# Zeros of 64 columns before the first K product, keys of 12 tiles summed on VectorE, and a new order, in a one-core linear-attention block with an MLP

## The chip, the cores and the metric

The kernel runs on one core of one Trainium2 chip. The metric is the device time of one execution in microseconds (us); lower is better. The five engines of the core each work through a queue of their own, in order: TensorE (PE, with its weight loads PEld), VectorE (DVE), ScalarE (ACT), GpSimd (POOL) and SyncE (SP), which issues all the DMAs here. Times inside an execution are counted from the start of its span.

## The reference

Input x is 2048 rows of 512 values in bfloat16. There are 32 heads of 16.

```python
def phi(t): return where(t > 0, t + 1, exp(t)) + 1e-6
u = layernorm(x)                          # over the 512 values of a row
q, k, v = split(u @ wqkv)                 # wqkv 512 x 1536
kv  = einsum("bhsd,bhse->bhde", phi(k), v)
z   = sum over s of phi(k)
o   = (phi(q) @ kv) / (phi(q) . z + 1e-6)
h   = x + o @ wo
out = h + relu(layernorm(h) @ w1) @ w2    # w1 512 x 1792, w2 1792 x 512
```

## The kernel before

The 2048 rows are 16 tiles of 128 rows; four tiles make a chunk c of 512 rows. Everything stays in SBUF. One string, ORDER (lines 18 to 53), fixes the order of the whole program: each word names a piece of work and its numbers, and the last loop of the kernel (lines 528 to 530) calls the function `op_<name>` with them. Words of one engine stand in that engine's queue in the order of the string; between engines only data count. There is no loop over tiles, and no scheduler.

The words that matter below (t a tile, c a chunk, b a PSUM bank):

- `lx.t.n` loads n tiles of x, `lk lq lv lo l1 l2` load parts of the weights (lines 200 to 211), all from SP's queue.
- `const` (line 173) sets constants on DVE, among them the zeros, and makes the identity on POOL; `masks` (186) makes masks on POOL. `warm.n.b` (213) multiplies zeros by zeros n times into bank b, 512 columns each, and nobody reads the result.
- `S.t`, `A.t` (218, 219): row statistics of x on DVE. `R.t.n` (238): 1/sqrt(variance) on ACT. `N.t` (241): normalized rows on DVE.
- The normalized tile is transposed in one of two ways. `T.t.b` (265) does it on PE, and `E.t` (ACT, 271) or `V.t` (DVE, 274) copies the result out of PSUM; `X.t` (283) does it with a DMA transpose. Tiles 0 to 3 take the first way, 4 to 15 the second.
- `K.t.b` (287): keys of tile t, 4 matmuls of 128x512. `F U M D` (329 to 332) make phi of them: exp and relu on ACT, a minimum and an add on DVE. `G.t` (341) adds u.T @ phi(k) of tile t into banks 4 to 7; v is never computed, its weights come in later.
- The sum z of the keys over all rows: `za.t` (348) adds the phi(k) of two tiles to an accumulator in float32 on DVE (1024 columns each time), `zf` (352) folds the two halves and splits them into two bfloat16 parts, and `z.j.b.t0` (358) sums over rows on PE by products with a column of ones: the two parts and the tiles t0 to 15, which were not added on DVE. `zc`, `zh` (367, 370) bring z to the form in which `dn` uses it.
- `Q.c.j.b` (296): queries of chunk c, with phi by `qF qU qM qD`. `gA`, `gD` (375, 378) copy the sums of G out of PSUM on ACT or DVE, `kv`, `kx` (381, 390) and `m` (394) turn them into one 512x512 matrix m, which `mA` or `mD` (398, 401) copies out.
- For each chunk a chain: `dn.c` (435, PE) the denominators, `dnl`, `dnx` (445, 451, ACT) their inverse spread over the heads, `dt.t` (458) four DMA transposes into rd, `dm.c` (462, DVE) phi(q) times rd, `h.t` (470, PE) times m, `hD` (479, DVE) plus x, `s a n` (220, 221, 249) the second layernorm's statistics and centred rows, `x.t` (284) four DMA transposes of these (hn) into lnT.
- The MLP: `p.c.f.b` (486, PE) a first product of 4 matmuls, `pA` or `pD` (495, 500) relu of two of them on ACT or DVE, `f.t.b.f0.n` (506, PE) n matmuls of the second product, `fo` (516, DVE) scale and add of h, `fd` (523) the store.

PSUM has 8 banks, and every word names its own.

Of the kernel before, what the change touches and what calls it, by code (L numbers as in the profile page):

```python
# [28 lines left out]
zc G.12 qD.0.0.2 G.13 zh dn.0.0 G.14 G.15 dnl.0 dnx.0.2.2 gD.0.2 Q.1.0.2 Q.1.1.3 dnx.0.0.2 gA.2.2 kv.0.4
Q.1.2.0 kv.3.4 Q.1.3.1 kv.2.4 qF.1.0.2 qU.1.0.2 qM.1.0.2 lo.2.2 lo.0.2 kv.1.4 kx Q.2.1.3 qF.1.2.2 dt.2 dt.3  # L30
dt.0 dt.1 qU.1.2.2 m.0.4 m.1.5 m.3.7 m.2.6 Q.2.0.2 qM.1.2.2 mA.0.2 qD.1.0.2 qD.1.2.2 dn.1.5 mA.2.2 dnl.1
dnx.1.2.2 dm.0.0.2 dm.0.2.2 h.3.4 h.2.0 hD.3 s.3 l1.0.2 dnx.1.0.2 hD.2 dt.6 a.3 Q.2.3.1 h.0.5 s.2 dt.4 hD.0
qU.2.0.2 qF.2.0.2 Q.2.2.0 qM.2.0.2 h.1.2 dt.5 dt.7 s.0 n.3 a.2 hD.1 a.0 s.1 n.0 Q.3.1.3 a.1 n.2 qF.2.2.2
qU.2.2.2 qM.2.2.2 dm.1.0.2 Q.3.0.2 dm.1.2.2 n.1 Q.3.3.1 Q.3.2.0 x.3 qF.3.0.2 qU.3.0.2 h.7.4 h.6.5 x.0 x.2
qU.3.2.2 qD.2.2.2 x.1 qD.2.0.2 dn.2.3 dnl.2 qF.3.2.2 h.5.6 h.4.7 hD.7 qM.3.0.2 hD.6 hD.5 s.7 p.0.0.2 p.0.1.3
hD.4 qM.3.2.2 s.6 dnx.2.2.2 dnx.2.0.2 pD.0.0.2 qD.3.2.2 s.4 dt.10 p.0.3.1 p.0.2.0 p.0.4.2 p.0.5.3 pA.0.2.2
pA.0.4.2 qD.3.0.2 dt.8 dt.11 dt.9 dn.3.6 p.0.6.0 p.0.7.1 p.0.13.3 dnl.3 s.5 a.4 p.0.12.2 pA.0.6.2 dnx.3.0.2
pA.0.12.2 r.0.4 dnx.3.2.2 l2.0.7 a.5 n.5 a.7 dm.2.0.2 a.6 n.6 dm.2.2.2 n.7 x.7 h.11.4 h.9.6 h.8.1 h.10.5 hD.11
n.4 hD.9 hD.8 hD.10 x.4 dt.13 dt.12 x.6 x.5 dt.14 dt.15 p.0.10.0 f.2.6.0.7 p.0.11.1 pA.0.10.2 p.0.8.2 p.0.9.3
f.3.7.0.7 pD.0.8.2 s.8 dm.3.0.2 dm.3.2.2 f.2.6.7.7 p.1.0.0 p.1.1.1 f.3.7.7.7 h.12.3 pD.1.0.2 h.14.4 p.1.2.2  # L40
p.1.12.0 hD.12 s.12 fo.3 fo.2 s.10 a.12 s.9 hD.14 s.11 a.9 n.9 h.13.7 f.1.5.0.7 p.1.13.1 h.15.3 a.10 hD.13 a.8
n.10 pD.1.12.2 n.8 hD.15 s.15 p.1.10.6 p.1.11.7 f.0.4.0.7 p.1.3.3 p.1.8.0 f.0.4.7.7 a.15 p.1.9.1 fd.2
f.1.5.7.7 pD.1.2.2 s.13 n.15 pA.1.8.2 fo.1 a.11 n.12 n.11 pD.1.10.2 x.8 x.9 x.10 x.11 p.1.4.0 p.1.5.1 p.1.6.2
r.4.4 p.1.7.3 pA.1.4.2 pA.1.6.2 f.5.5.0.7 p.2.3.3 p.2.8.0 p.2.9.1 f.7.7.0.7 p.2.2.2 pD.2.8.2 fo.0 p.2.1.1
p.2.0.0 f.6.6.0.7 s.14 a.13 n.13 pD.2.2.2 pD.2.0.2 a.14 p.2.7.3 f.4.4.0.7 p.2.12.0 p.2.6.2 f.7.7.7.7 p.2.13.1
n.14 f.5.5.7.7 pD.2.6.2 pA.2.12.2 p.2.5.1 p.2.4.0 x.13 fd.0 fd.3 x.15 fd.1 pA.2.4.2 x.14 x.12 f.4.4.7.7
p.3.0.0 p.3.2.2 p.3.1.1 f.6.6.7.7 p.3.3.3 pA.3.2.2 pD.3.0.2 fo.7 fo.5 fo.6 fo.4 p.3.9.1 f.11.7.0.7 p.2.11.3
fd.4 p.3.8.0 p.2.10.2 f.9.5.0.7 pD.2.10.2 pD.3.8.2 p.3.6.2 p.3.7.3 f.9.5.7.7 f.10.6.0.7 pA.3.6.2 p.3.10.2
p.3.11.3 f.8.4.0.7 fd.6 fd.5 fd.7 p.3.4.0 f.10.6.7.7 p.3.5.1 f.11.7.7.7 f.8.4.7.7 pA.3.4.2 r.12.4 r.8.4
pD.3.10.2 fo.9 fo.10 fo.8 fo.11 p.3.12.0 p.3.13.1 pD.3.12.2 fd.9 fd.8 fd.10 fd.11 f.14.6.0.7 f.13.5.0.7  # L50
f.12.4.0.7 f.14.6.7.7 f.13.5.7.7 f.12.4.7.7 fo.13 fo.14 fo.12 fd.12 fd.14 f.15.7.0.14.0.2 fo.15.0.2
f.15.4.0.14.2.1 f.15.5.0.14.3.1 fo.15.2.1 fo.15.3.1 fd.13 fd.15.0.2 fd.15.2.1 fd.15.3.1
"""


# [1 line left out]
def kernel(  # L57
# [155 lines left out]
    def op_warm(n, b):  # L213
        for _ in range(n):
            nc.tensor.matmul(bk[:, b, :], lhsT=zeros[:, 0:P], rhs=zeros, start=True, stop=True)
# [345 lines left out]
```

## Time and profile before

| | us |
|---|---|
| median of 3 runs | 171.17 |
| the three runs | 171.17, 172.66, 170.6 |
| the profiled execution | 171.47 |
| its span, first to last instruction | 169.8 |
| PE busy | 162.2 |
| DVE busy | 103.3 |
| ACT busy | 64.9 |
| POOL busy | 4.7 |
| time to the first K product | 7.30 |
| time to the first MLP product (p.0.0) | 62.62 |

The sizes of the pieces by the profile's groups (mean of one instruction): a row statistic on DVE 0.67, an aggregate 0.16, a normalization 0.40, a copy or relu of 128x1024 out of PSUM 1.22 on DVE and 1.02 on ACT, an add of 128x1024 into the accumulator 1.22. DMA transposes take a median of 2.5 us from issue to landing.

How to read it: a group's line gives engine, operation, shape, count, then busy time, the mean of one in nanoseconds, and the idle time before it with what ended most of it. A row of the order of time gives start, length, engine, line, names and count, with the idle time before it in brackets. A PE instruction's length holds its way through the array, so the distance from one start to the next, and not the length, is what it costs.

### The profile page before, as it was taken

The numbers are of one execution on the slowest core, as the hardware profiler recorded it, in microseconds if no ns is written. First come the engines' busy times: TensorE is split into PE (matmuls) and PEld (weight loads), VectorE is DVE, ScalarE is ACT, GpSimd is POOL, SyncE is SP. The second block draws the span as 40 slices with busy tenths as digits, with TensorE's granted clock in tenths as the row PEclk, the third lists the DMA queues.
The fourth block names the chain that finished last, engine by engine and source line by source line (L and its number), as shares of the span: only waits on it lengthen the run. The fifth ranks groups of instructions, "written<-read, shape, count | busy, mean of one in ns | idle before, by whom it ended". The sixth has DMA issues, their size and how long they took to land.

```text
span 169.8 us, 2263 instructions
## 1 busy us (share of the span) xinstructions
PE 162.2 (96%) x843; PEld 75.4 (44%) x858; DVE 103.3 (61%) x206; ACT 64.9 (38%) x97; POOL 4.7 (3%) x21
## 2 busy tenths in 40 slices
...
GB/s 144 251 253 95 94 95 184 262 359 60 99 174 165 93 66 85 152 173 86 92 6 31 31 62 29 2 0 107 113 0 0 70 54 4 0 0 124 0 4 120
DMA packets 32234, 15.87 MB, mean 93 GB/s; under 512 B 24800, under 2 KB 31200, under 8 KB 32224
## 3 DMA queue, kind: packets, MB, share of 16 engines
...
q8 instruction: 6, 0.10, 0.2%
q14 instruction: 4, 0.03, 0.1%
HBM read 7.86 MB, written 2.10 MB: 59 GB/s over the span
## 4 chain that ended last, share of the span: by engine, by line
PE 80%; DMA 6%; DVE 6%; SPq 2%; issue 2%; ACT 1%; DVEq 0%
PE bk L510 29%; PE bk L490 28%; PE bk L474 7%; PE bk L343 7%; PE bk L291 5%; PE bk L299 5%; DMA x_nat<-in_A_x_dram 3%; DMA lnT<-h_nat 2%; DVE h_nat L480 2%; DMA rd<-wk_sb 1%; SPq L201 1%; DVE st L220 1%; DVE h_nat L243 1%; PE bk L440 1%; ACT eb L309 1%
## 5 line engine op out<-in xcount | busy, mean ns | idle before, releaser
L510 PE MATMUL bk<-w_sb,at 128*128 128x512 bf16 (+2 forms) x249 | 51.9, 355 | 0.2
L490 PE MATMUL bk<-lnT,w_sb 128*128 128x512 bf16 x219 | 51.8, 379 | 0.2
L496 ACT ACTIVATE at<-bk 128x1024 bf16<-128x1024 f32 x13 | 13.3, 1024 | 70.6 <-PE bk L490 48.7
L501 DVE TENSOR_SCALAR at<-bk 128x1024 bf16<-128x1024 f32 x15 | 18.2, 1220 | 32.5 <-PE bk L490 32.3
L510 PEld LDWEIGHTS <-at 128*128 128x128 bf16 x252 | 23.6, 98 | 25.4 <-ACT at L496 0.3
L490 PEld LDWEIGHTS <-w_sb 128*128 128x128 bf16 x224 | 21.8, 98 | 26.1 <-issue 0.2
L518 DVE SCALAR_TENSOR_TENSOR gT<-bk,rstd,h_nat 128x512 bf16<-128x512 f32 (+2 forms) x18 | 11.7, 685 | 16.0 <-PE bk L510 10.5
L312 ACT ACTIVATE rb<-bk 128x1024 bf16<-128x1024 f32 (+1 forms) x18 | 16.4, 927 | 3.7 <-PE bk L299 2.4
L309 ACT ACTIVATE eb<-bk 128x1024 bf16<-128x1024 f32 (+1 forms) x18 | 16.6, 927 | 3.0 <-PE bk L299 2.8
L291 PE MATMUL bk<-wk_sb,lnT 128*128 128x512 bf16 x63 | 15.6, 379 | 1.3 <-DMA wk_sb<-in_A_wqkv_dram 0.6
L474 PE MATMUL bk<-m_sb,pqs 128*128 128x512 bf16 x61 | 15.0, 379 | 0.9 <-DVE pqs L464 0.8
L299 PE MATMUL bk<-lnT,wq_sb 128*128 128x512 bf16 x64 | 15.6, 379 | 0.2 <-DVE h_nat L480 0.2
L343 PE MATMUL bk<-at,h_nat 128*128 128x512 bf16 x54 | 13.3, 379 | 0.1
L480 DVE TENSOR_TENSOR h_nat<-bk,x_nat 128x512 bf16<-128x512 f32 x16 | 10.9, 681 | 2.0 <-PE bk L474 1.9
L218 DVE BATCH_NORM_STATS2 st<-x_nat 128x6 f32<-128x512 bf16 x16 | 10.6, 674 | 2.4 <-DMA x_nat<-in_A_x_dram 2.4
L220 DVE BATCH_NORM_STATS2 st<-h_nat 128x6 f32<-128x512 bf16 x16 | 11.0, 686 | 0.1
L291 PEld LDWEIGHTS <-lnT 128*128 128x128 bf16 x64 | 5.8, 98 | 9.5 <-DMA lnT<-h_nat 1.8
L474 PEld LDWEIGHTS <-pqs 128*128 128x128 bf16 x64 | 6.0, 98 | 8.0 <-DVE pqs L464 1.5
L299 PEld LDWEIGHTS <-wq_sb 128*128 128x128 bf16 x64 | 6.1, 98 | 7.2 <-issue 0.4
L343 PEld LDWEIGHTS <-h_nat 128*128 128x128 bf16 x64 | 6.1, 98 | 7.1
L316 DVE TENSOR_SCALAR eb<-eb 128x1024 bf16<-128x1024 bf16 (+1 forms) x18 | 6.8, 384 | 2.5 <-ACT eb L309 2.5
L453 ACT ACTIVATE wk_sb<-ld 128x1024 bf16<-128x1024 f32 x8 | 8.1, 1049 | 0.1
...
## 6 DMA issues: line engine op xcount, KB each, us to landing
...
```

Of the source, the lines that this page charges most:

```text
L220: op_s = lambda t: nc.vector.bn_stats(out=st2[:, t, :], in_=h_nat[:, t, :])
L291: nc.tensor.matmul(bk[:, b, :], lhsT=lnT[c][:, kd, j * P : (j + 1) * P], rhs=wk_sb[:, kd, :], start=(kd == 0), stop=(kd == KD - 1),)
L299: nc.tensor.matmul(bk[:, b, :], lhsT=wq_sb[:, kd, j * P : (j + 1) * P], rhs=lnT[c][:, kd, :], start=(kd == 0), stop=(kd == KD - 1),)
L309: nc.scalar.activation(out=buf(eb, kind, i, n), in_=bank(at_bank[kind, i], n), func=ACT.Exp)
L312: nc.scalar.activation(out=buf(rb, kind, i, n), in_=bank(at_bank[kind, i], n), func=ACT.Relu)
L343: nc.tensor.matmul(bk[:, KD + kd, :], lhsT=ln_nat[:, t, kd * P : (kd + 1) * P], rhs=pk(t)[:, 0, :], start=(t == 0), stop=(t == NT - 1),)
L474: nc.tensor.matmul(bk[:, b, :], lhsT=pqs[:, (c * KD + jb) % NQ, j * P : (j + 1) * P], rhs=m_sb[:, jb, :], start=(jb == 0), stop=(jb == KD ...
L480: nc.vector.tensor_tensor(out=h_nat[:, t : t + n, :], in0=bank(at_bank["h", t], n), in1=x_nat[:, t : t + n, :], op=ALU.add,)
L490: nc.tensor.matmul(bk[:, b, cols], lhsT=w1_sb[:, kd, f * P : (f + 1) * P], rhs=lnT[c][:, kd, cols], start=(kd == 0), stop=(kd == KD - 1),)
L496: nc.scalar.activation(out=acts[c % 2][:, f : f + n, :], in_=bank(at_bank["p", c, f], n), func=ACT.Relu)
L501: nc.vector.tensor_scalar(out=acts[c % 2][:, f : f + n, :], in0=bank(at_bank["p", c, f], n), scalar1=0.0, scalar2=None, op0=ALU.max,)
L510: nc.tensor.matmul(bk[:, b, 0 : w * P], lhsT=acts[c % 2][:, f, j * P : (j + 1) * P], rhs=w2_sb[:, f, k * P : (k + w) * P], start=(f == 0), ...
```

## The change

- New word `warms.n.b`: n products of zeros of 64 columns. 48 of them are added: 16 ahead of the ten long zeros, which stay, 16 behind them and ahead of the first transpose T.0, and 16 between T.0 and T.2.
- The accumulator on DVE takes 12 tiles in place of 14: `za.12` is gone, and the four `z` words start at tile 12, so that each has 6 products in place of 4.
- The order is new everywhere. At the start: the loads of x go 2, 1, 0, 4 and 5, 3 in place of 0, 2, 1, 3, 4 and 5; the transposes on PE go 0, 2, 1, 3 in place of 2, 0, 1, 3, and tile 2 is copied out by DVE (`V.2`) and not by ACT. The loads of the two halves of w1 swap places. `gA.2` becomes `gD.2`, `mA.2` becomes `mD.2`, and some relus of the MLP go from DVE to ACT or back. The banks are new, too.

```diff
-const lx.0.1 S.0 lx.2.1 S.2 lx.1.1 A.2 A.0 table warm.9.7 R.2.1 S.1 lx.3.1 N.2 A.1 R.0.1 R.1.1 N.0 lx.4.2
-warm.1.7 T.2.0 S.3 E.2 N.1 T.0.1 A.3 lk.0.2 lk.2.2 S.4 S.5 A.4 lx.6.2 A.5 T.1.5 E.0 R.3.1 E.1 R.4.2 lx.8.4 N.3
-K.0.3 S.6 N.4 F.0.1 U.0.1 K.1.0 lx.12.4 M.0.1 S.7 N.5 F.1.1 X.4 A.6 D.0.1 M.1.1 A.7 T.3.5 E.3 K.2.3 S.9 U.1.1
...
-K.14.2 K.15.3 qU.0.0.2 qF.0.0.2 za.10 G.9 za.12 Q.0.2.0 Q.0.3.1 F.14.2 l1.2.2 M.14.2 U.14.2 zf.12 qF.0.2.2
-D.14.2 G.10 G.11 z.0.2.14 z.2.2.14 z.1.2.14 qM.0.2.2 qM.0.0.2 z.3.2.14 qU.0.2.2 qD.0.2.2 lv.2.2 l2.7.7 lv.0.2
...
+lx.2.1 const lx.1.1 lx.0.1 S.2 S.1 A.2 masks S.0 A.1 table lx.4.2 A.0 lx.3.1 R.2.1 R.0.1 R.1.1 N.2 S.3 N.0 A.3
+S.4 N.1 S.5 lk.0.2 warms.8.2 warms.8.1 warm.9.7 warm.1.7 warms.8.3 warms.8.2 A.4 T.0.4 warms.8.1 warms.8.5
+T.2.0 R.3.1 A.5 E.0 T.1.6 V.2 lk.2.2 K.0.5 E.1 R.4.2 K.1.1 lx.6.2 N.3 S.7 N.5 A.7 N.4 U.0.1 T.3.0 F.0.1
+lx.12.4 lx.8.4 M.0.1 E.3 X.5 X.4 K.2.3 S.6 D.0.1 A.6 F.1.1 U.1.1 K.3.0 M.1.1 R.6.2 D.1.1 N.6 G.0 N.7 S.9 F.2.1
+S.8 M.2.1 F.3.1 U.3.1 U.2.1 X.6 A.8 A.9 G.1 D.2.1 K.5.1 R.8.2 K.4.0 S.12 M.3.1 G.2 N.9 N.8 D.3.1 X.7 F.4.2 X.8
...
+lv.2.2 l2.7.7 lv.0.2 G.10 K.14.2 lo.0.2 lo.2.2 Q.0.2.0 G.11 Q.0.3.1 G.12 U.14.2 F.14.2 qF.0.2.2 zf.10 M.14.2
+D.14.2 qM.0.0.2 z.2.2.12 z.3.2.12 z.1.2.12 z.0.2.12 G.13 qD.0.0.2 qU.0.2.2 qM.0.2.2 zc zh qD.0.2.2 G.14 dn.0.0
+G.15 Q.1.0.2 Q.1.1.3 dnl.0 gD.2.2 gD.0.2 Q.1.2.0 kv.3.4 Q.1.3.1 dnx.0.0.2 dnx.0.2.2 qF.1.0.2 qU.1.0.2 dt.1
+dt.3 dt.2 dt.0 qM.1.0.2 kv.0.4 kv.2.4 kv.1.4 qF.1.2.2 qD.1.0.2 Q.2.1.3 qU.1.2.2 kx m.1.5 m.0.4 qM.1.2.2
+qD.1.2.2 m.3.7 m.2.6 mD.2.2 dm.0.0.2 Q.2.2.0 mA.0.2 dn.1.5 dm.0.2.2 Q.2.0.2 h.3.7 h.0.6 hD.3 h.2.7 dnl.1
+dnx.1.2.2 dnx.1.0.2 qF.2.0.2 qU.2.0.2 s.3 Q.2.3.1 hD.0 hD.2 a.3 Q.3.1.3 h.1.5 Q.3.0.2 s.0 n.3 a.0 s.2 n.0
+l1.2.2 a.2 qF.2.2.2 qU.2.2.2 dt.7 hD.1 n.2 dt.5 dt.6 dt.4 s.1 dm.1.0.2 dm.1.2.2 a.1 Q.3.3.1 qM.2.0.2 qF.3.0.2
+qU.3.0.2 Q.3.2.0 n.1 h.5.6 h.4.4 h.7.7 qM.2.2.2 qF.3.2.2 qD.2.0.2 x.3 qD.2.2.2 x.0 x.2 x.1 qU.3.2.2 qM.3.0.2
+dn.2.3 qD.3.0.2 qM.3.2.2 qD.3.2.2 hD.5 dnl.2 h.6.5 hD.4 hD.7 dnx.2.0.2 dt.8 dnx.2.2.2 p.0.2.0 p.0.3.1 dn.3.6
...
+    def op_warms(n, b):
+        for _ in range(n):
+            nc.tensor.matmul(bk[:, b, 0:64], lhsT=zeros[:, 0:P], rhs=zeros[:, 0:64], start=True, stop=True)
+
```

In the changed kernel the functions stand 5 lines lower from line 218 on (and 1 line lower before that).

More of the change, by code (lines that the diff above doesn't have):

```diff
@@ L29 @@
[L29 to L52, printed above, removed]
+lx.2.1 const lx.1.1 lx.0.1 S.2 S.1 A.2 masks S.0 A.1 table lx.4.2 A.0 lx.3.1 R.2.1 R.0.1 R.1.1 N.2 S.3 N.0 A.3
@@ new lines @@
+qU.3.0.2 Q.3.2.0 n.1 h.5.6 h.4.4 h.7.7 qM.2.2.2 qF.3.2.2 qD.2.0.2 x.3 qD.2.2.2 x.0 x.2 x.1 qU.3.2.2 qM.3.0.2
+dn.2.3 qD.3.0.2 qM.3.2.2 qD.3.2.2 hD.5 dnl.2 h.6.5 hD.4 hD.7 dnx.2.0.2 dt.8 dnx.2.2.2 p.0.2.0 p.0.3.1 dn.3.6
+dt.11 dt.10 dt.9 l2.0.7 dnl.3 pA.0.2.2 p.0.0.2 p.0.1.3 pA.0.0.2 r.0.4 s.7 s.5 dm.2.0.2 p.0.6.0 p.0.13.4
+p.0.5.3 p.0.4.2 p.0.7.1 dnx.3.2.2 pA.0.6.2 dm.2.2.2 s.4 dt.14 dt.15 h.9.6 h.8.7 h.11.0 dnx.3.0.2 p.0.11.1 hD.6
+s.6 a.4 n.4 hD.9 s.9 dt.13 a.5 a.7 pA.0.4.2 hD.11 hD.8 n.5 a.6 dt.12 n.6 a.9 dm.3.0.2 h.10.5 p.0.12.3 x.5
```

23 lines of the change are left out of this document (18 added, 5 removed).

## The prediction

> **What bounds the kernel now.** I read the page first (shares, chain, queues), then who waited for whom on PE, then the order of time on PE and on the DMA-issuing queue SP. The profiled execution took 171.47 us: a span of 169.8 and 1.7 around it.
>
> ```profile
> span 169.8 us, 2263 instructions
> ...
> PE 162.2 (96%) x843; PEld 75.4 (44%) x858; DVE 103.3 (61%) x206; ACT 64.9 (38%) x97; POOL 4.7 (3%) x21
> ...
> q8 instruction: 6, 0.10, 0.2%
> ...
> PE 80%; DMA 6%; DVE 6%; SPq 2%; issue 2%; ACT 1%; DVEq 0%
> ```
>
> TensorE is the bound: 96% busy, 80% of the chain. So only PE's waits, its first 8 us and the 2.9 us after its last matmul can change. PE's waits:
>
> ```profile
> PE bk L215 <- DVE ones L177: 1.2, 1, 1.2
> PE bk L474 <- DVE pqs L464: 0.8, 1, 0.8
> PE bk L291 <- DMA wk_sb<-in_A_wqkv_dram: 0.6, 1, 0.6
> PE bk L291 <- DMA lnT<-h_nat: 0.5, 1, 0.5
> PE bk L262 <- DVE h_nat L243: 0.5, 1, 0.5
> PE bk L299 <- DVE h_nat L480: 0.2, 1, 0.2
> ```
>
> From the first K product on they are few and short. PE in order of time, at the start and around the worst wait:
>
> ```profile
> 1.25 4.45 PE L215 MATMUL bk<-m_sb 128*128 128x512 bf16 x10 [1.25 <-DVE ones L177]
> 5.68 0.78 PE L262 MATMUL bk<-ident,h_nat 128*128 128x128 bf16 x8
> 6.98 0.40 PE L262 MATMUL bk<-ident,h_nat 128*128 128x128 bf16 x4 [0.52 <-DVE h_nat L243]
> 7.30 0.60 PE L291 MATMUL bk<-wk_sb,lnT 128*128 128x512 bf16 x2
> 8.54 0.81 PE L291 MATMUL bk<-wk_sb,lnT 128*128 128x512 bf16 x3 [0.63 <-DMA wk_sb<-in_A_wqkv_dram]
> ```
>
> ```profile
> 48.49 0.55 PE L440 MATMUL bk<-zhd,pqT 128*128 128x8 bf16 x16
> 49.84 1.84 PE L474 MATMUL bk<-m_sb,pqs 128*128 128x512 bf16 x7 [0.81 <-DVE pqs L464]
> ...
> 56.16 2.75 PE L299 MATMUL bk<-lnT,wq_sb 128*128 128x512 bf16 x12 [0.16 <-DVE h_nat L480]
> ...
> 62.62 0.59 PE L490 MATMUL bk<-lnT,w_sb 128*128 128x512 bf16 x2
> ```
>
> The zeros cost 0.43 us each, later 128x512 matmuls 0.216: PE starts at half speed and is at full speed by the transposes (0.057 each). K.0 starts at 7.30 but stops for the second half of wk until 8.54. Start-to-start distances above 0.216 lost from 7.30 to the end: 0.8 (wk), 0.25 and 0.12 (K.2, K.3), 0.7 (K.7, a transposed tile), 0.2 (K.11), 0.1, 1.1 (h.3), 0.3 (56.16): some 3.5 us. From 62.62 (the first MLP product) to 166.9 PE never waits. So the point to compare is when the MLP starts: 62.62 before.
>
> SP issues the DMA transposes one after the other:
>
> ```profile
> 41.40 6.19 SPq L460 DMA_TRANSPOSE rd<-wk_sb  x4
> ...
> 50.71 5.12 SPq L460 DMA_TRANSPOSE rd<-wk_sb  x4
> 55.92 5.15 SPq L284 DMA_TRANSPOSE lnT<-hn  x4
> ```
>
> Four take 5.1 us; the four from 41.40 took 6.19, and h.3's wait hangs on them. Just then (44.68 in the trace's packet records) one of the six 16 KB packets of q8 ran. They start at 21.97, 44.68, 63.33, 88.23, 115.85 and 142.85, after 88, 226, 342, 472, 601 and 728 weight loads of PE: about one per 128 load-and-matmul pairs, so I take them for PE's instructions. The transpose issued at 21.27 took 2.08 us in place of 1.22, the one at 43.99 2.28, the one at 115.91 2.68, the one at 63.32 1.48: a collision costs 0.3 to 1.5 us.
>
> **The start.** Removed: nothing. Added ahead of K.0: 48 pairs of 64 columns. Pairs of 128x8 or 128x1 run 0.025 apart, 128x128 0.057, 128x512 0.216; the line through the last two gives 0.031 for 64 columns, 0.053 at half speed (0.427/8). The ends are 0.025 and 0.107 (a 128-column pair at half speed); I take the line, as 64 lies between the rows.
>
> What decides is DVE, in order (a bn_stats each 0.60, aggregate 0.09, normalization 0.32 apart; a result is there after 0.68, 0.16, 0.40). First tile lands at 3.01 as before: S.2 3.04, S.1 3.65, A.2 4.26, S.0 4.35, A.0 done 5.22, N.2 5.15 to 5.55. S.3 needs tile 3, now loaded behind the two-tile load; the fifth load landed at 6.06. So S.3 6.05, N.0 done 7.03 (6.01 before), S.4, N.1 done 8.05. PE: 16 zeros to 2.1, the ten long ones to 6.0 (full speed from 5.6), 16 to 6.5, T.0 at 7.08 to 7.3, 16 zeros to 7.8, T.2, T.1 8.1 to 8.33, K.0 at 8.33. No zero delays a transpose at these prices; at 0.107 in every place K.0 would come later (below). K.0 starts 1.0 later, but the stop for wk is gone (its third matmul falls at 8.76, wk was there at 8.50): K.0 ends at 9.2 against 9.4.
>
> Then K.1 9.2 (E.1 9.15), T.3 10.06, K.2, K.3 11.25 (waits 0.1 for E.3), G.0 12.1 (D.0 done 12.05; V.2, now on DVE at about 0.6, half of the 1.22 of the 128x1024 copy, is in it), G.1, K.5, K.4, G.2 15.5 (D.2), K.6, G.3 to 18.1. These are 11 products; before, the 11th (K.7) ended at 18.9. Gain 0.8. Against it: 48 more pairs bring the first q8 packet 48 pairs of work sooner, to G.0, about 12.5, where the transposes X.5 and X.4 (issued 10.6 and 11.9) fly; K.4 then waits up to 0.6. Ends -0.8 and -0.2; I take **-0.5**.
>
> **Sums of keys.** One 128x1024 add (1.22) leaves DVE, 8 pairs of one column come to PE: 8 x 0.025 = **+0.2**, on the path. The add frees nothing: z waits for D.14, behind F.14 on ACT, which ends at about 36.1 with or without it; without that cover it would be worth 1.2. Copies moved from ACT to DVE: gD.2 and gD.0 in a row 2.44, under three Q products of 2.59, then 0.2 to land: +0.1. Masks move on POOL, which nobody waits for (used at 46); the two halves of w1 swap places on SP, both long before 62: nothing.
>
> So dn.1 starts at 48.49 - 0.5 + 0.3 = 48.3.
>
> **h.3.** From dn.0 the chain dnl, dnx, four transposes, dm took 2.07 to the first issue, then 3.8 and 2.45 to land without a collision: 8.3; dn.0 lies 8.3 before dn.1 and h.3 1.3 behind it. The second q8 packet moves to the z products (37 to 38), where no transpose flies. So rd is there as dn.1 starts, mD.2.2 ends on DVE at 48.9, dm.0.0 49.6, dm.0.2 50.2, h.3 at 49.6 with 0.2 lost in place of 1.1: **-0.9**.
>
> **What is late next.** The order gives less cover to the chains after it. From dn.1: transposes of rd issued from +2.2, landed +8.55 (before: 57.04 - 48.49); dm.1.2 done +9.95; h.5, now 9.3 behind dn.1 (h.7 was 10.3), loses 0.25. Then four transposes of hn: x.1 landed +13.85 before; p.0.2 stands 13.35 behind dn.1 (products after dn.1 counted at 0.862, small pairs at 0.025, and the losses above): waits to +13.9. The third q8 packet (44 to 56 pairs of work sooner than 63.33) falls at about 52.7 to 53, among these eight transposes: +0.3 to +1.0, I take +0.7. p.0.2 starts at 48.3 + 13.9 + 0.7 = 62.9, against 62.62. The bank wait at 56.16 (0.3) is counted as covered by this chain.
>
> **After it** 104.1 us of products in both; order and banks leave slack wherever I looked, least at p.2.3, whose last transpose x.10 stands behind an output store and lands 0.3 to 0.7 ahead, with the fifth q8 packet near: 0 to 0.7, I take 0. The last 2.9 us are the same.
>
> Sum: 171.47 + (62.9 - 62.62) = 171.75. The median of the three runs is 0.3 below the profiled one: **171.4**.
>
> On the packets, the Trainium skill (Runtime: NRT & Kernel Launch, Instruction fetch mechanics) says that instructions come in 16 KiB blocks of 256, which agrees with 128 pairs, and that the cost of a block is mostly hidden. By that the 0.7 falls away and the sum is 171.05; here the four issues of 6.19 against 5.12 say otherwise.
>
> **The rivals.** (B) The chains are not hit: the start gains 0.8, no q8 packet meets a transpose, x.1 lands as DVE's words allow. Then dn.1 at 48.0, p.0.2 at 61.3 to 61.9: 169.9 to 170.5. For it: only four of six packets met a transpose. Against: eight transposes in a row fill 10 of the 14 us after dn.1.
>
> (C) The other side: zeros in the way of the transposes, with PE at half speed. PE works in order, and 32 of the 48 short pairs stand in front of T.0 and 16 in front of T.2. If short matmuls do not count as work and each takes 0.107: long zeros end at 7.2, T.0 8.9, T.1 done 12.0, K.0 +3.7, and two K products at half speed +1.7: 171.4 + 5.4 = 176.8. It decides (174.6) once K.0 starts 3.2 late, after 11.5 (after 9.8 with both K slow). For it: no row shows what 64 columns do to the speed. Against: speed came by 5.6 in 4.4 us of zeros, and the ten long zeros (4.3 us) are still there.
>
> The Trainium skill (TensorE: Matmul & The Clock Gate, Part 1) has the clock open after one busy window of about 3.4 us that runs freely; PE busy without a gap from 1.25 would then be at full speed by 8.1 at the latest, (C) would cost 1.2 and end at 172.6. The 4.4 us here agree with it.
>
> (D) Several collisions: K.4 +0.6, the dm and x chain +1.0, x.10 +0.7, all ends taken: dn.1 48.6, p.0.2 63.5, MLP +0.7: 172.1 to 172.8; with the bank wait of 56.16 still there, 173.1.
>
> **Numbers.** Forecast 0.50 (170.7 with the start's better end and a packet of 0.3, 172.1 with the worse and 1.0), B 0.20, D 0.20, C 0.08, and 0.02 that orders save more than the 3.5 us of waits listed. Range 169.9 to 173.1: it leaves out C, the 0.02 and some of D's end. Two per cent (167.7 to 174.6) is about what a measurement of this kernel can tell from no change. Faster needs more than all of PE's waits: 0.02. Slower is C and a little of D: 0.10. The rest, 0.88, is within.
>
> **What would show it.** The first K product at 8.3 without a stop for wk; 64-column pairs 0.03 to 0.055 apart, none running when a normalization is done; z with 24 pairs in 0.6; no wait over 0.3 at the first h product; PE waiting on pqs or transposed hn between 57 and 63; q8 packets at about 12.5, 37.5 and 53, and a group of four transposes there over 5.5 us; the MLP starting at 62.9. Wrong if K.0 comes after 9, if the MLP waits later on, or if it starts before 61.5.

## The result

The changed kernel takes 173.51 us (median of 6 runs, 172.78 to 174.0); the kernel before, on the same chip, 171.23 (6 runs). The ratio is 1.0114 with a 95% interval of 1.0066 to 1.0162: slower by about 1%, where 171.4 was forecast and 173.1 was the end of the range. The profiled execution took 173.65 us with a span of 171.9; the one before 171.47 and 169.8.

The page of the changed kernel (its span, its engines, its packet queue, the chain by engine):

```profile
span 171.9 us, 2390 instructions
...
PE 164.5 (96%) x914; PEld 77.4 (45%) x914; DVE 105.0 (61%) x207; ACT 63.9 (37%) x95; POOL 4.9 (3%) x21
...
q8 instruction: 7, 0.11, 0.3%
q14 instruction: 4, 0.03, 0.1%
...
PE 81%; DMA 10%; SPq 3%; DVE 2%; issue 2%; ACT 1%; DVEq 0%
```

PE is as full as before, so the shares say nothing of the loss; but DMA's share of the chain has grown from 6 to 10%, and q8 has seven packets where it had six. A second queue of instructions, q14, has four packets of 8 KB, as many as before; it comes up again below. Who waited for whom, on PE:

```profile
PE bk L296 <- DMA lnT<-h_nat: 1.0, 1, 1.0
PE bk L479 <- DVE pqs L469: 0.7, 1, 0.7
...
PE bk L495 <- DMA lnT<-hn: 0.5, 1, 0.5
PE bk L348 <- DVE pk_lo L324: 0.4, 1, 0.4
```

The stop for wk is gone. The wait for a DMA transpose of x is 1.0 at K.5, where it was 0.5 at K.6, and the one for pqs 0.7 at h.5, where it was 0.8 at h.3. New are a wait for D.0 (at G.0) and one ahead of the MLP. PE in order of time, at the start and around the MLP's begin:

```profile
2.10 4.23 PE L216 MATMUL bk<-m_sb 128*128 128x512 bf16 x10
6.17 0.63 PE L221 MATMUL bk<-m_sb 128*128 128x64 bf16 x16
7.35 0.40 PE L267 MATMUL bk<-ident,h_nat 128*128 128x128 bf16 x4 [0.55 <-DVE h_nat L248]
...
8.57 1.89 PE L296 MATMUL bk<-wk_sb,lnT 128*128 128x512 bf16 x8
...
12.80 1.89 PE L348 MATMUL bk<-pk_lo,h_nat 128*128 128x512 bf16 x8 [0.39 <-DVE pk_lo L324]
15.69 1.90 PE L296 MATMUL bk<-wk_sb,lnT 128*128 128x512 bf16 x8 [1.00 <-DMA lnT<-h_nat]
```

```profile
49.68 0.55 PE L445 MATMUL bk<-zhd,pqT 128*128 128x8 bf16 x16
...
51.23 3.01 PE L479 MATMUL bk<-m_sb,pqs 128*128 128x512 bf16 x12
...
60.15 2.93 PE L479 MATMUL bk<-m_sb,pqs 128*128 128x512 bf16 x12 [0.72 <-DVE pqs L469]
...
64.82 1.89 PE L495 MATMUL bk<-lnT,w_sb 128*128 128x512 bf16 x8 [0.48 <-DMA lnT<-hn]
```

The 64-column zeros hold up no K product: the last 16 end at 8.05, and T.1, the last transpose ahead of K.0, needs N.1, done at 8.28. K.0 stands near where the forecast had it (8.57 for 8.33). But dn.1 begins at 49.68 (48.49 before) and the MLP at 64.82 (62.62 before). From there to the last matmul it is 104.01 us in the one and 104.05 in the other. So all of the 2.2 us come ahead of the MLP, in two parts. A mark that both kernels have is the start of the last product of G.15: it is at 41.24 before and at 42.42 after (+1.18), and the MLP begins 21.38 behind it before and 22.40 after (+1.02).

SP's queue shows both parts. Its rows have the start, the time that the issues take, and their number:

```profile
11.26 15.47 SPq L288 DMA_TRANSPOSE lnT<-h_nat  x10
...
43.43 5.12 SPq L465 DMA_TRANSPOSE rd<-wk_sb  x4
...
51.85 6.18 SPq L465 DMA_TRANSPOSE rd<-wk_sb  x4
58.13 5.15 SPq L289 DMA_TRANSPOSE lnT<-hn  x4
```

The ten transposes of x take 15.47 and start at 11.26; before it was 14.38 from 10.27. The four of rd that were hit before (6.19) are free now, and the next four, free before (5.12), are hit: 6.18. The q8 packets start at 12.4, 42.54, 55.55, 79.0, 108.1, 133.3 and 158.5. The first falls on X.5 (issued at 11.26, landed at 15.65, 4.39 later, when 2.5 is the usual), the third on the last two of the four.

### The profile page after: what moved, and what is told of

It reads as the page before. It is cut to its first block, busy times and chain, and to the rows that moved or that the text cites. A ratio compares the mean times of both kernels' runs of the same rounds, so it can differ in the third digit from the quotient of the medians.

```text
span 171.9 us, 2390 instructions
## 1 busy us (share of the span) xinstructions
PE 164.5 (96%) x914; PEld 77.4 (45%) x914; DVE 105.0 (61%) x207; ACT 63.9 (37%) x95; POOL 4.9 (3%) x21
## 4 chain that ended last, share of the span: by engine, by line
PE 81%; DMA 10%; SPq 3%; DVE 2%; issue 2%; ACT 1%; DVEq 0%
PE bk L495 28%; PE bk L515 28%; PE bk L348 7%; PE bk L296 6%; PE bk L304 5%; PE bk L479 4%; DMA x_nat<-in_A_x_dram 4%; DMA lnT<-h_nat 3%; DMA rd<-wk_sb 2%; DMA lnT<-hn 1%; SPq L202 1%; SPq L465 1%; DVE pqs L469 1%; PE bk L445 1%; ACT wk_sb L458 1%
## 5 line engine op out<-in xcount | busy, mean ns | idle before, releaser
L515 PE MATMUL bk<-w_sb,at 128*128 128x512 bf16 (+2 forms) x252 | 51.2, 355 | 0.0
L501 ACT ACTIVATE at<-bk 128x1024 bf16<-128x1024 f32 x14 | 14.1, 1020 | 76.1 <-PE bk L495 76.1
L506 DVE TENSOR_SCALAR at<-bk 128x1024 bf16<-128x1024 f32 x14 | 17.0, 1221 | 30.4 <-PE bk L495 30.4
L495 PEld LDWEIGHTS <-w_sb 128*128 128x128 bf16 x224 | 21.8, 98 | 26.9 <-issue 0.9
L523 DVE SCALAR_TENSOR_TENSOR gT<-bk,rstd,h_nat 128x512 bf16<-128x512 f32 (+2 forms) x18 | 12.2, 686 | 18.6 <-PE bk L515 18.5
L479 PE MATMUL bk<-m_sb,pqs 128*128 128x512 bf16 x64 | 15.9, 379 | 0.9 <-DVE pqs L469 0.7
L469 DVE TENSOR_TENSOR pqs<-pqT,rd 128x1024 bf16<-128x1024 bf16 x8 | 5.2, 688 | 4.9 <-DMA rd<-wk_sb 4.8
```

What stands on the lines that cost most here:

```text
L479: nc.tensor.matmul(bk[:, b, :], lhsT=pqs[:, (c * KD + jb) % NQ, j * P : (j + 1) * P], rhs=m_sb[:, jb, :], start=(jb == 0), stop=(jb == KD ...
L495: nc.tensor.matmul(bk[:, b, cols], lhsT=w1_sb[:, kd, f * P : (f + 1) * P], rhs=lnT[c][:, kd, cols], start=(kd == 0), stop=(kd == KD - 1),)
L501: nc.scalar.activation(out=acts[c % 2][:, f : f + n, :], in_=bank(at_bank["p", c, f], n), func=ACT.Relu)
L506: nc.vector.tensor_scalar(out=acts[c % 2][:, f : f + n, :], in0=bank(at_bank["p", c, f], n), scalar1=0.0, scalar2=None, op0=ALU.max,)
L515: nc.tensor.matmul(bk[:, b, 0 : w * P], lhsT=acts[c % 2][:, f, j * P : (j + 1) * P], rhs=w2_sb[:, f, k * P : (k + w) * P], start=(f == 0), ...
L523: nc.vector.scalar_tensor_tensor(out=o_t[:, t % NO, cols], in0=bk[:, at_bank["f", t, k], 0 : w * P], scalar=rstd2[:, t : t + 1], in1=h_nat ...
```

## The experiments

"Cover" below is the work that PE still has in hand while a result is on its way. Theories: **P**, the packets: 48 more pairs move the q8 packets into transposes that PE waits for. **O**, the order: the new order itself is longer, wherever the packets fall. **Z**, the zeros: they stand in the way, or cost by themselves. The table has the runs whose parts are compared (e2 and e6 stand in the text alone): the first K product, the last product of G.15, the distance to the MLP, the distance to the last matmul, the first three packets, the ratio to the kernel before on the same chip.

| run | K.0 | G.15 | to MLP | to last | packets | ratio (95%) |
|---|---|---|---|---|---|---|
| before | 7.30 | 41.24 | 21.38 | 104.05 | 22.0, 44.7, 63.3 | 1 |
| after | 8.57 | 42.42 | 22.40 | 104.01 | 12.4, 42.5, 55.6 | 1.0114 (1.0066 to 1.0162) |
| e4, before with 58 pairs | 7.62 | 41.85 | 22.74 | 104.12 | 12.7, 39.6, 57.2 | 1.0075 (1.0038 to 1.0111) |
| e7, before with 87 | 7.28 | 40.91 | 21.35 | 104.06 | 10.3, 37.0, 50.3 | 0.9999 (0.9968 to 1.003) |
| e1, no short zeros | 8.68 | 42.38 | 21.36 | 104.73 | 24.4, 42.7, 64.8 | 1.0148 (1.011 to 1.0186) |
| e3, all zeros short | 8.77 | 42.91 | 21.32 | 104.71 | 7.2, 24.9, 43.3 | 1.0126 (1.008 to 1.0171) |
| e5, after with 79 | 8.54 | 42.36 | 22.00 | 105.14 | 11.0, 39.2, 53.0 | 1.0112 (1.0068 to 1.0156) |
| e8, 14 tiles on DVE | 8.80 | 42.99 | 22.54 | 104.01 | 12.8, 42.0, 58.8 | 1.0155 (1.0109 to 1.0201) |
| e9, changed start only | 7.87 | 41.84 | 23.27 | 104.22 | 13.0, 42.1, 56.8 | 1.0137 (1.0084 to 1.0189) |
| e10, changed rest only | 7.42 | 41.91 | 21.01 | 104.79 | 21.8, 46.4, 65.1 | 1.002 (0.9983 to 1.0056) |
| e11, rest only, 87 | 7.63 | 41.40 | 21.63 | 104.90 | 10.2, 37.5, 51.2 | 1.0052 (1.0019 to 1.0085) |
| e12, tile 3 sooner | 7.80 | 42.56 | 22.36 | 104.01 | 11.7, 42.7, 55.8 | 1.0135 (1.0091 to 1.0179) |
| e13, S.7 later | 8.25 | 42.11 | 22.39 | 104.01 | 13.2, 42.5, 55.3 | 1.0096 (1.0064 to 1.0128) |
| e14, both | 8.03 | 42.59 | 22.23 | 104.01 | 13.8, 43.1, 56.7 | 1.0065 (1.0032 to 1.0097) |
| e15, after with 93 | 9.20 | 44.25 | 21.89 | 104.01 | 11.6, 34.2, 54.8 | 1.0145 (1.01 to 1.0191) |
| e16, e14 with 93 | 7.93 | 43.41 | 22.05 | 104.01 | 11.5, 33.6, 54.1 | 1.0123 (1.0085 to 1.0161) |
| e17, e7, wk sooner | 7.32 | 41.61 | 21.70 | 104.06 | 9.3, 37.7, 51.5 | 1.0013 (0.9976 to 1.005) |

Single starts vary by some tenths with the landing of the loads: e7 and e11 have the same program up to G.15, and differ by 0.5 there.

### The zeros taken away, and their number changed

**e1_no_short**: the 48 short zeros are taken out.

```diff
-lk.0.2 warms.8.2 warms.8.1 warm.9.7 warm.1.7 warms.8.3 warms.8.2 A.4 T.0.4 warms.8.1 warms.8.5
+lk.0.2 warm.9.7 warm.1.7 A.4 T.0.4
```

> The changed kernel without its 48 pairs of 64 columns; the ten long zeros stay. Theory P (the 48 extra pairs bring PE's instruction packets onto DMA transposes): the packet leaves 12.4 us and falls 48 pairs of work later, near 18 to 19, where the tiles under way have 2 us of cover; K.5 no longer waits to 15.7, the 11 first products end 1.0 to 1.5 earlier than 20.0, and the third packet moves from 55.5 to about 64, so that the four transposes from 51.9 take 5.1 and not 6.2; the second may meet the chain ahead of the first h product (+0.5): 171.3 to 172.3. Theory O (the new order has less cover at the start and after dn.1, whatever the packets do): as the changed kernel, 173.2 to 173.8. Theory Z (the short zeros stand in the way or keep the speed up): K.0 starts earlier or runs slower than 8.57, and the time moves by that alone.

Measured 174.37, ratio 1.0148. PE in order of time:

```profile
7.30 1.59 PE L267 MATMUL bk<-ident,h_nat 128*128 128x128 bf16 x12 [1.60 <-DVE h_nat L248]
8.68 2.74 PE L296 MATMUL bk<-wk_sb,lnT 128*128 128x512 bf16 x8
11.26 0.39 PE L267 MATMUL bk<-ident,h_nat 128*128 128x128 bf16 x4
```

Z falls: K.0 is not sooner without the zeros (8.68), and its products run at half speed until 10.39 (T.3 starts 2.58 behind K.0, where the changed kernel has 1.73). So the short zeros did keep the clock: in e1 PE has 1.60 us without a product in their place. P's mechanism is seen: without a packet X.5 lands 2.64 behind its issue (4.39 in the changed kernel), the four transposes of dt take 5.12 (6.18), the wait for pqs is gone and the MLP is 21.36 behind G.15. But the packets go elsewhere: the third falls at 64.8 on the four behind the MLP's begin (6.07), and from the MLP to the last matmul it is then 104.73, 0.7 more; little cover there in this order would explain it. SP's rows:

```profile
51.86 5.12 SPq L465 DMA_TRANSPOSE rd<-wk_sb  x4
57.07 5.16 SPq L289 DMA_TRANSPOSE lnT<-hn  x4
63.99 6.07 SPq L465 DMA_TRANSPOSE rd<-wk_sb  x4
```

**e2_six_long**: eight short zeros are replaced by one long each time (16 pairs of zeros).

```diff
-warms.8.2 warms.8.1 warm.9.7 warm.1.7 warms.8.3 warms.8.2 A.4 T.0.4 warms.8.1 warms.8.5
+warm.1.2 warm.1.1 warm.9.7 warm.1.7 warm.1.3 warm.1.2 A.4 T.0.4 warm.1.1 warm.1.5
```

> The changed kernel with each group of 8 short zeros made one zero product of 512 columns: the same time on the array, 42 pairs fewer. Theory P: as the kernel without the short zeros, within 0.4 us, because only the count of instructions matters: 171.3 to 172.3. Theory O: as the changed kernel. Theory Z: as the changed kernel, since PE works on zeros for as long.

Measured 176.38, ratio 1.0248 (1.0192 to 1.0303); the packet came at 21.65 on X.9, and PE had 2.15 us without a product. PE in order of time, and then a stretch behind the wait (its bounds, its length, the busy time of PE, PEld, DVE, ACT and POOL, the granted clock, the DMA share and GB/s):

```profile
21.05 1.03 PE L296 MATMUL bk<-wk_sb,lnT 128*128 128x512 bf16 x4
24.23 1.04 PE L296 MATMUL bk<-wk_sb,lnT 128*128 128x512 bf16 x4 [2.15 <-DMA lnT<-h_nat]
25.10 4.44 PE L348 MATMUL bk<-at,h_nat 128*128 128x512 bf16 x12
```

```profile
25.30:28.60 3.30, 3.30 (x9) 1.18 (x8) 1.69 (x5) 1.94 (x2) 0.00 (x0) 0.50 0.52 85
```

The clock was then at half for 3.41 us (25.27 to 28.68): G.15 starts at 45.73, 3.3 us behind the changed kernel's. This run is no measure of the order.

**e3_all_short**: all zeros short, 138 pairs, so that the packets behind the first stand as with 10.

```diff
-warm.9.7 warm.1.7
+warms.80.7 warms.10.7
```

> The changed kernel with the ten long zeros made 90 short ones: 138 zero pairs in all, 128 (one packet's worth) more than in the kernel without short zeros. Theory P: the packets fall at the same work as there, so the time is the same as there within 0.4 us, 171.3 to 172.3, and earlier than the changed kernel in spite of 80 more pairs. Theory Z: zeros cost or the speed suffers, slower than the changed kernel, over 174. Theory O: as the changed kernel.

Measured 174.03, ratio 1.0126, with the packets of e1 one place on (24.9, 43.3, 65.3), a stop of 0.83 at K.0 for wk, which landed at 9.99, and the clock at full speed from 4.2. The packet at 7.2 falls in the loads; that it made wk late is not shown, as wk was nearly as late without one in e5 (9.61) and e14 (9.40).

**e5_after_79**: three long zeros replaced by 24 short ones.

```diff
-warm.9.7 warm.1.7
+warms.24.7 warm.6.7 warm.1.7
```

> The changed kernel with three of its ten long zeros made 24 short ones: 79 zero pairs for 58, the same time on the array. Theory P (PE's instruction packets, one about every 128 pairs, delay the DMA transposes that they meet): 21 pairs sooner, the first packet falls near 8 (loads, not transposes), the second near 35, the third near 50.6, the fourth near 73.7. The transpose for K.5 lands 2.6 after its issue and not 4.4, K.5 waits 0 to 0.4 in place of 1.2; the four transposes after dn.1 take 5.1 and h.5 waits 0.3 in place of 0.9; the loads or the first h product may lose 0.5: 171.3 to 172.6. Theory O (the new order as such): 173.2 to 173.8.

Measured 173.99, ratio 1.0112. K.5 waits no more (X.5 landed 2.8 behind its issue), but G.15 is where it was, 42.36: K.0 stops 0.67 for wk, and K.9 waits 0.92 for X.9, until 22.54. The packet at 53.0 still meets the four transposes of dt (5.81). So the packets of q8 alone do not account for the changed kernel: none of the other places tried for them in this order is clearly better than its own ratio of 1.0114 (e1, e2, e3, e5 and e15: 1.0112 to 1.0248).

### The kernel before with more pairs

**e4_before_58** and **e7_before_87** have the order before, and zeros of 64 columns in the time of long ones: only the number of pairs ahead of T.2 changes, from 10 to 58 and to 87. (The expectations of e10, e11 and e17 speak of 17 long zeros; there are ten.)

```diff
 e4                                    e7
-table warm.9.7 R.2.1                 -table warm.9.7 R.2.1
+table warm.3.7 warms.27.2 R.2.1      +table warms.40.7 warms.20.2 R.2.1
-warm.1.7 T.2.0                       -warm.1.7 T.2.0
+warms.27.1 warm.1.7 T.2.0            +warms.27.1 T.2.0
```

> The kernel before with its order as it was; of its ten long zeros six become 54 short ones, 58 pairs and about the same time ahead of the first transpose. Theory P: 48 pairs sooner, the first packet meets the transposes of tiles 4 to 7 (near 13) and the K product that needs them waits 0.5 to 1.5 more; the second leaves the four transposes that took 6.19, so the first h product waits 0.1 and not 1.1; the third falls at 52 to 56 among the next eight, +0.7 to 1.0: 171.3 to 172.7. Theory O: as the kernel before, 171.0 to 171.5, with the packets moved but nothing waiting for them.

> The kernel before with its ten long zeros made 87 short ones, about the same time. Theory P: packets near 6 (loads; the stop for wk may last up to 1 longer), 33, 49.5 and 72: none meets the four transposes ahead of the first h product (its wait of 1.1 goes to 0.1) nor the eight after dn.1; the MLP starts 0 to 1 sooner than 62.6: 170.3 to 171.8, although it has 77 pairs more. If only more PE instructions cost: slower than with 58 pairs, over 173.5.

e4 took 173.47 (1.0075), e7 171.44 (0.9999): the intervals do not meet. The same products in the same order cost nothing, or 1.3 us by the ratios (1.9 by the medians), by where the packets fall. SP's rows of e4, then of e7, for the four transposes of dt and the four of hn:

```profile
51.32 5.13 SPq L464 DMA_TRANSPOSE rd<-wk_sb  x4
56.54 6.29 SPq L288 DMA_TRANSPOSE lnT<-hn  x4
```

```profile
50.37 5.33 SPq L464 DMA_TRANSPOSE rd<-wk_sb  x4
55.80 5.16 SPq L288 DMA_TRANSPOSE lnT<-hn  x4
```

In e4 the packet at 57.2 meets the last transpose of rd in flight (landed at 59.51) and the transposes of hn behind it, and PE waits:

```profile
60.38 2.07 PE L478 MATMUL bk<-m_sb,pqs 128*128 128x512 bf16 x8 [1.54 <-DVE pqs L468]
```

P is shown as a mechanism: the hit is worth 1.4 us between G.15 and the MLP (22.74 against 21.35 and 21.38), and e4's first packet, at 12.66 on X.4 and X.5, makes K.4 wait 0.65. And the pairs cost nothing by themselves: e7 has 77 more than the kernel before.

**e6_before_38** is a third place, with 38 pairs.

```diff
-table warm.9.7 R.2.1
+table warm.3.7 warms.16.2 R.2.1
-warm.1.7 T.2.0
+warms.16.1 warm.3.7 T.2.0
```

> The kernel before with its ten long zeros made 6 long and 32 short ones: 28 pairs more in the same time. Theory P: the first packet falls near 15 (tiles 7 to 9; K.7 already waits 0.7 there, up to 1 more), the second near 39, so that the first h product waits 0.1 and not 1.1, the third near 60, on the last transposes ahead of the MLP, which then waits 0.7 to 1.0: 171.0 to 172.5, between the kernel before and the one with 58 pairs (173.5). Theory O: 171.0 to 171.7.

Measured 172.66, ratio 1.0063 (1.0029 to 1.0097): slower than the kernel before, and not to be told from e4. Its trace is of an execution of 174.97, far from its median, and is not used.

### The sum of the keys

**e8_after_z14**: the changed order, with 14 tiles added on VectorE again.

```diff
-zf.10 M.14.2 D.14.2 qM.0.0.2 z.2.2.12 z.3.2.12 z.1.2.12 z.0.2.12
+za.12 zf.12 M.14.2 D.14.2 qM.0.0.2 z.2.2.14 z.3.2.14 z.1.2.14 z.0.2.14
```

> The changed kernel with 14 tiles summed on DVE again: one add of 128x1024 (1.2) more on DVE, ahead of the fold, and 8 pairs fewer at z. The prediction's claim that the add is covered: as the changed kernel, -0.2 to +0.2, 173.2 to 173.8. Theory S (in the new order the fold ends as F.14 does, so the add has no cover): D.14 and the z products come 1.1 later, PE waits 1.0 there, 174.3 to 174.8.

Measured 174.55, ratio 1.0155. The products of z now wait for D.14, which VectorE reaches later by the add in front of it; PE in order of time:

```profile
39.51 0.55 PE L367 MATMUL bk<-ones,at 128*128 128x1 bf16 x16 [1.01 <-DVE at L324]
```

The changed kernel has no wait there. D.14 ends at 39.45, 38.88 in the changed kernel, and VectorE has no idle time ahead of it from the add on. So the removed add is worth 0.6 us or more in this order, up to the wait of 1.17, and "the add frees nothing" was wrong; in the times the two intervals overlap.

### Half of the order at a time

**e9_start_only** has the changed order up to G.15 and the one before from there; **e10_rest_only** the reverse; **e11_rest_only_87** is e10 with 87 pairs.

```diff
 e9:  changed order up to G.15, then   dnl.0 dnx.0.2.2 gD.0.2 Q.1.0.2 ...   (before)
 e10: order before up to G.15, then    Q.1.0.2 Q.1.1.3 dnl.0 gD.2.2 ...     (changed)
```

> The changed kernel's order up to and with G.15 (its zeros, its loads, 12 tiles on VectorE), and from there the order of the kernel before (lo is loaded in the first part, l1.2 in the second). If the changed start alone loses time that never comes back: the last product of G.15 at 42.4 as in the changed kernel (41.2 before), the MLP 21.4 (no q8 packet among the transposes after it) to 22.4 (one among them) behind it, at 63.8 to 64.8: 172.6 to 173.7. The packet due at 55.5 would fall at the end of the four transposes of dt or the first of hn, so I take 173.3. If the second half of the order is to blame for more than the packet: back at 171.5 to 172.

> The order before up to and with G.15 with its ten long zeros first and seven more behind, as before, and from there the changed order (lo loaded just ahead of G.15). If the loss sits in the start and in the packet that its zeros move into the transposes of dt: the last product of G.15 at 41.2, packets at 22, 44.5 and 63, none among the four transposes of dt (50 to 55.5) and of hn (to 61), the MLP 21.4 or a little less behind G.15, at 62.3 to 62.6: 171.1 to 171.6. If the changed second half is itself worse (less cover: it waits 0.5 to 0.6 ahead of the MLP in every run of it): 172.2 to 173.

> As the run before this one, with 87 pairs of 64-column zeros in the time of the 17 long ones. The packets come 77 pairs sooner, at about 10.3, 37 and 50. If only collisions count: the one at 50 falls just before or on the first transpose of dt.4, G.15 ends at 40.9 and the MLP starts at 62.2 to 62.8: 170.9 to 171.7, so at best the same as before. If the packet is on the group: up to 172.5.

e9 takes 174.07 (1.0137), e10 172.31 (1.002), e11 172.95 (1.0052). In e10 the changed rest loses nothing that can be told, and from G.15 to the MLP it is even the shortest of all, 21.01; e11 loses 0.5%, with its third packet on the four transposes of dt (5.73). The changed start alone loses 0.6 us up to G.15 in this run and 1.9 behind it. Of the 1.9, a wait of 0.7 is the seam's own (PE waits there for ACT's copy of gT, as neither kernel does); the rest is that its zeros put the third packet (56.8) on the four transposes of dt. SP's rows of e9:

```profile
52.15 6.20 SPq L462 DMA_TRANSPOSE rd<-wk_sb  x4
58.44 5.16 SPq L286 DMA_TRANSPOSE lnT<-hn  x4
```

In e10 the third packet meets the four behind the MLP's begin: 104.79 from there to the last matmul, 0.7 more. Before, a packet that began with these four (63.33, issues of 5.41) cost nothing; whether the cover is less in the changed order or the hit was smaller, no run shows. SP's row:

```profile
63.28 6.00 SPq L462 DMA_TRANSPOSE rd<-wk_sb  x4
```

### What is long in the changed start

**e12_tile3_sooner** swaps two loads, **e13_s7_later** moves S.7, A.7 and S.6 on VectorE, **e14_s7_tile3** does both.

```diff
 e12 and e14
-table lx.4.2 A.0 lx.3.1 R.2.1
+table lx.3.1 A.0 lx.4.2 R.2.1
 e13 and e14
-lx.6.2 N.3 S.7 N.5 A.7 N.4 U.0.1
+lx.6.2 N.3 N.5 N.4 U.0.1
-K.2.3 S.6 D.0.1 A.6 F.1.1
+K.2.3 S.7 D.0.1 A.7 S.6 A.6 F.1.1
```

> The changed kernel with one swap: tile 3 is loaded ahead of tiles 4 and 5, as before the change. If K.0 is late (8.57 against 7.30) because S.3 waits for tile 3 (landed 6.28): S.3 at about 5.3, K.0 at 7.5 to 7.7, and the start gains 0.5 to 0.9 up to G.15 if it isn't given back: 172.6 to 173.0. If the transposes X.4 and X.5, which wait for tiles 4 to 7 and the packet, set the start instead: K.0 sooner, longer waits at K.5 and K.7, G.15 at 42.2 to 42.5 and 173.3 to 173.6.

> The changed kernel with VectorE's words S.7 and A.7 moved behind N.5, N.4 and M.0 (S.7 ahead of D.0, A.7 and S.6 behind it); nothing else. If S.7's wait for its tiles, with N.5 and N.4 queued behind it, makes the start late: X.5 issued at 10.0 to 10.4 in place of 11.26, the wait of 1.17 us at K.5 down to 0.2 at most, G.0 without its wait of 0.55, the last of G.15 0.8 to 1.4 sooner, at 41.0 to 41.6; with the packet of 55.55 still in the four transposes of dt: 172.1 to 172.8. If the packet at 12.4 or the clock or K.0 sets the start: G.15 stays at 42.2 to 42.6, and 173.3 to 173.8.

> As the run before, and tile 3 is loaded ahead of tiles 4 and 5. If S.7 was what ate the 0.8 us that K.0 gained from the sooner tile: X.5 issued at 9.3 to 9.6, the last of G.15 at 40.4 to 41.0, and 171.4 to 172.2 with the packet still among the transposes of dt. If K.0 counts for nothing in any case: as the run before, within 0.2.

e12: 174.17 (1.0135). K.0 starts at 7.80, and the gain is gone by G.0, which waits for D.0: VectorE stands at S.7 until tiles 6 and 7 have landed at 10.62, with D.0 queued behind it. Then K.9 waits for X.9. VectorE and PE in order of time:

```profile
10.65 0.69 DVE L223 BATCH_NORM_STATS2 st<-x_nat 128x6 f32<-128x512 bf16 x1 [1.69 <-DMA x_nat<-in_A_x_dram]
...
22.74 1.04 PE L296 MATMUL bk<-wk_sb,lnT 128*128 128x512 bf16 x4 [0.57 <-DMA lnT<-h_nat]
```

e13: 173.83 (1.0096). X.5 is issued at 9.94, 1.3 sooner, and lands at 15.34, as late as before the move: the loads of x are still running (to 13.33) and the packet comes at 13.18; which of the two held it is not shown. K.5 waits on; PE in order of time:

```profile
15.38 1.90 PE L296 MATMUL bk<-wk_sb,lnT 128*128 128x512 bf16 x8 [0.91 <-DMA lnT<-h_nat]
```

e14: 173.31 (1.0065); G.15 at 42.59, with a stop of 0.98 for wk, which landed at 9.40. The intervals of e13, e14 and the changed kernel overlap, and so do those of e12 and the changed kernel: neither K.0 nor S.7 alone is the place.

The traces say what holds this start. In e1, e3, e5, e12 and e14 PE waits at K.9 for X.9, until 22.54 to 23.08, and in all five the last product of G.15 starts 19.82 or 19.83 behind K.9. In the changed kernel X.9 lands at 22.47 and K.9 starts at 22.61, without a wait, and the last product of G.15 follows 19.81 later. So two delays end there together: K.5's wait for X.5 and the late landing of X.9. Taking away the first alone would have gained about 0.1 us, an estimate from these rows.

X.9 takes 3.40 to 3.49 us from issue to landing in these six and in e8, e13, e15 and e16, where 2.4 to 2.5 is usual, and each time a packet of q14 begins while it flies (at 20.94 in the changed kernel). In e9 this packet (20.55) comes when X.9 is all but there, and X.9 takes 2.47. In the order before, the packet comes at 16.5 to 17.2, on X.6, which takes 3.2 to 3.6 and is waited for at K.6 (before, e4, e7, e10, e11, e17). The zeros move the packets of q8; this one stayed on X.9 in each of e1, e2, e3 and e5. Whose instructions q14 brings, no run shows.

### Both packets elsewhere, and wk sooner

**e15_after_93** replaces five long zeros by 40 short ones, **e16_s7_tile3_93** does so in e14, **e17_before_87_wk** loads wk ahead of tiles 4 and 5 in e7.

```diff
 e15 and e16
-warm.9.7 warm.1.7
+warm.5.7 warms.40.7
 e17
-R.1.1 N.0 lx.4.2
+R.1.1 N.0 lk.0.2 lk.2.2 lx.4.2
```

> The changed kernel with five of its long zeros replaced by 40 of 64 columns in the same time, so 93 pairs of zeros in place of 58. The packets come about 35 pairs sooner: at 10 to 10.5 (ahead of X.5), 36.5 to 38, 49.5 to 51 (ahead of the four transposes of dt). If packets on transposes are the loss: no wait of 1.2 at K.5, the four transposes of dt take 5.1, the last of G.15 at 41.6 to 42.1, the MLP 21.0 to 21.4 behind it, at 62.7 to 63.4, and 171.4 to 172.4 unless a later packet meets the transposes of dt.8 or the next hn (then 0.7 more). If the changed order itself is worse by more than that: 173 or more.

> As the run before, with S.7 behind N.5, N.4 and M.0 and tile 3 loaded sooner. With the packets out of the way the sooner transposes should count: 0.3 to 0.8 less than the run before, 171.0 to 171.9. If the loads of x hold X.5 anyway: the same as the run before.

> The kernel before with 87 zeros of 64 columns in place of the 17 long ones (that was 171.44), and wk loaded ahead of tiles 4 and 5. K.0 loses its stop of 0.7 for wk; S.4 and S.5 may come up to 0.5 later. If the stop is worth what it shows: 170.7 to 171.2, ahead of both kernels. If the tiles 4 and 5 that come later cost it again at K.4 to K.7: 171.3 to 171.8.

e15: 175.02 (1.0145); e16: 174.16 (1.0123). The packets did not come where I wanted them: the second at 34.2 met X.14, which landed 4.20 behind its issue, the third at 54.8 the four of dt. PE of e15 in order of time:

```profile
34.41 1.03 PE L348 MATMUL bk<-at,h_nat 128*128 128x512 bf16 x4
36.52 1.04 PE L296 MATMUL bk<-wk_sb,lnT 128*128 128x512 bf16 x4 [1.09 <-DMA lnT<-h_nat]
```

So these two say nothing of the order without hits. e17: 172.53 (1.0013, 0.9976 to 1.005), no gain: K.0 and K.1 run through, but tiles 4 and 5 land at 7.95 (6.13 in e7), VectorE stands 0.91 at S.4 with N.3 queued behind, and PE waits 0.6 at T.3 and 0.8 at K.2 instead; VectorE in order of time:

```profile
7.98 1.29 DVE L222 BATCH_NORM_STATS2 st<-x_nat 128x6 f32<-128x512 bf16 x2 [0.91 <-DMA x_nat<-in_A_x_dram]
```

No version tried is faster than the kernel before.

## Why the prediction was wrong

The step that failed is **the start**, "Gain 0.8 ... Against it ... K.4 then waits up to 0.6 ... I take -0.5". In its place stood +1.0 us: G.15 is 1.18 later, of which 0.2 are the products of z. The sum stopped at the eleventh product, at 18.1, took one collision, and put at nothing every wait between there and G.15. K.9 stands three products further on, so at 20.7 by the forecast's own steps (21.0 with the 0.3 of the collision); X.9 landed at 22.47, and K.9 started at 22.61 (20.63 before, with one product less ahead of it). By its steps:

- The 64-column pairs (0.053 and 0.03 apart), K.0 at 8.33 without a stop for wk: 8.57, right but for 0.24, since tile 3 landed at 6.26 and not at 6.06.
- G.0 at 12.1: 12.80. I had S.7 in VectorE's queue without asking when tiles 6 and 7 land. They landed at 10.20 (9.22 before), VectorE idled 0.50, and N.5, N.4 and D.0 stand behind. X.5 was issued at 11.26 (10.6 forecast).
- The first packet "at about 12.5" on X.5 and X.4: at 12.40, right. Its price was too small: a wait of 1.17 at K.5 where "up to 0.6" stood. Without this wait X.9 would still have held K.9.
- X.9 was issued at 19.03 (17.34 before), behind N.8, which VectorE ended at 17.55 (15.78 before): tiles 6 and 7 landed 0.98 later, and VectorE worked without a pause from there to N.8, 7.32 us where it was 6.54. The packet of q14 added about 1.0 in flight. No run moves N.8 or that packet alone, so these shares are read from the traces.
- "K.0 ends at 9.2 against 9.4" is a misreading: K.1 followed at 8.97 before, and in the changed kernel at 9.43. The wait taken for K.7's before is K.6's.
- The gain itself, "the stop for wk is gone", did not come through: K.0's 1.27 us of delay were never regained. From K.0 to the last of G.15 it is 33.94 us before and 33.85 after; in e5, e12, e13 and e14 it is 33.82 to 34.76, however the waits are spread. I counted PE's waits as losses that a new order could take out one by one, and did not look which load or transpose came next.

"The add frees nothing" was wrong as well (e8), but it left the sum right, as z waits for nothing in the changed kernel; the +0.2 of z is right (24 products from 39.02 to 39.62). gD at +0.1 was 0: from G.15 to dn.1 it is 7.25 before and 7.26 after. h.3 at -0.9 was some -0.65 (0.45 lost in place of 1.1): mechanism right.

**What is late next** was right in kind and short in size: the third packet on the transposes, h.5 and then the MLP waiting. The forecast had the MLP 14.6 behind dn.1; it is 15.14 (14.13 before). The hit cost 1.06 on the four transposes, above the end of 1.0 that I gave; the packet came at 55.55, later than "52.7 to 53".

The 104.1 us behind it are right (104.01), the tail too. The sum: 1.4 us at dn.1 and 0.5 to the MLP are the 1.9 us between the 171.75 forecast for the profiled execution and its 173.65.

Rival C is refuted by K.0 at 8.57, by e1, and by e3, where short zeros alone have the clock at full speed from 4.2. D was the right one in kind; its end, 173.1, stopped short because all its cases kept the gain of the start.

The Trainium skill (Runtime: NRT & Kernel Launch, Instruction fetch mechanics) has the cost of an instruction block mostly hidden; by that the sum was 171.05. The trace disagrees: X.5 took 4.39 with a packet and 2.64 without, and e4 against e7 is 1.3 us by the ratios for the place of the packets.

The Trainium skill (TensorE: Matmul & The Clock Gate, Part 1) closes the clock after an idle window of about 3.4 us. In e2 2.15 us without a product were enough; that it stayed at half for 3.41 us agrees with one window.

What stays open: how long the changed start would be without hits. The changed kernel, e1, e3, e5, e9 and e12 to e14 have G.15 at 41.84 to 42.91 (mean 42.4), the kernel before, e4, e7, e10, e11 and e17 at 40.91 to 41.91 (mean 41.5), 0.9 us apart. A run of the changed order in which no packet meets a transpose was tried and not reached, so the first part, about 1.2 us, is read from the traces; the second, about 1.0, is shown by e4 against e7 and agrees with e1, e3 and e10, where it is gone. Why tiles 6 and 7 mostly land later with the changed start (9.24 to 11.06, before 9.06 to 9.84) is open. Why the second packet came at 42.5 and not at the 38 that the count gives is open, too.
